# Sliding-window attention before a gated feed-forward: key blocks from token 0, and probabilities added in pairs before they are summed

## The chip, the cores and the metric

The kernel runs on one NeuronCore of a Trainium2 chip: TensorE (matrix products into PSUM), ScalarE (activations), VectorE (element by element), GpSimd (which here issues loads), SyncE (which here issues stores and DMA transposes), SBUF, and PSUM of 8 banks of 128 x 512 float32. The metric is the device time of one execution in microseconds; the median of the runs counts.

## What is computed

Eight batches of eight heads, 576 tokens, 64 values per head. A token sees itself and the 127 tokens before it, with a bias that falls with the distance. The attention output of all batches, 4608 rows of 512, goes through a feed-forward of width 1536 with a GELU gate.

```python
scores = scale * np.matmul(q, k.transpose(0, 1, 3, 2))
rel = pos[:, None] - pos[None, :]
mask = (rel >= 0) & (rel < 128)
scores = np.where(mask, scores + bias, -1e9)
attn = np.exp(scores - max) / sum
x = (attn @ v) -> rows of 512
g = x @ w_gate
out = (gelu(g) * (x @ w_val)) @ w_out
```

## The kernel before

The work order of every engine is written out by hand; a tile's buffer is handed on in the order in which buffers were released.

**Attention, per batch.** q and k stand transposed (qT, kT: values on partitions, two heads of a pair c in the two halves i of 64 rows). Key block j covers tokens 128j - 64 to 128j + 63, so block 0 is half empty, and there are five. `score` (L191) makes keys-by-queries products; two heads of a pair run side by side in TensorE. A batch is split into two parts of its queries, s = 0 (320 tokens) and s = 1 (256). `scores2` (L204) does the 128 queries of block 2 that belong to part 0, `scores` (L220) the rest, for given pairs c; each pair takes two banks. ScalarE takes the exponential (L199), VectorE multiplies by the stored mask and bias `emask` (L202). `sums` (L313 to 323) adds the probabilities over keys with a matrix of ones, four pairs in four column strips of TensorE, then a reciprocal (L323). `products` and `values` (L351, L367) make probabilities times v, and VectorE multiplies by the spread reciprocal into xT, which holds all 4608 tokens. The reciprocals are spread over 64 partitions by a float32 matmul with a selection matrix (`spread_pe`, L339, batches 1 and 2; `spread4`, batch 0) or through DRAM (`gather`, `spread_dma`, from batch 3).

**Feed-forward, per group g of 512 tokens.** `gate_val(g, f)` (L387 to 402) makes feature block f of 12: eight matmuls into two banks, GELU on ScalarE (L400), product on VectorE (L401). `out_half` (L411) makes half of 128 output rows. A gate phase is the 12 blocks; the output phase that follows runs through the list `todo[g]`, eight output halves with attention steps of batch g + 2 between them (g = 0 does the whole of batch 1; g = 1 the whole of batch 2 and the scores of batch 3). From g = 2 the sums and values of batch g + 1 lie in the gate phase (L613 to 629; for g = 2 the values lie in the output phase).

**The start.** Batch 0 and 1 are transposed by TensorE (`transpose_runs`, L153), 320 and 256 tokens of batch 0 in two loads (`RUNS`). While data comes, `keep_busy` puts in matmuls of zeros (24 of them, L70). Group 0's first seven blocks are done for tokens 0 to 319 and then 320 to 511. Weights come in four steps of columns (256, 384, 384, 512), L460 to 464.

**Queues.** GpSimd issues every load of q, k, v and weights (L101, L128, L138, L554), in order. SyncE issues the DMA transposes of batches 2 to 7 (`transposes_dma`, L185; batch 2 from `todo[0]`, the others at the head of a gate phase, L601) and the stores of the output (L424). A one-element copy, `mark`, lets GpSimd wait for something before it goes on with loads: at g = 1 (L604) for batch 3's qT, ahead of the loads of batch 4. Batch 3's q and k and batch 2's v are loaded after gate phase 0, ahead of `todo[0]` (L633), with no mark.

Of the kernel before, what the change touches and what calls it, by code (L numbers as in the profile page):

```python
# [13 lines left out]

PART = ((0, 320), (320, 576))

PIECES = (((0, 0, 192), (1, 64, 320), (2, 192, 320)),
          ((2, 0, 128), (3, 0, 256), (4, 128, 256)))  # L20


PCOL = ({0: 64, 1: 256}, {4: 0, 2: 128, 3: 256})
# [3 lines left out]
def kernel(  # L27
# [12 lines left out]
    W = 128  # L40
# [10 lines left out]
    p_pool = (ctx.enter_context(tc.tile_pool(name="pa", bufs=8)),  # L51
              ctx.enter_context(tc.tile_pool(name="pb", bufs=4)))
    p2_pool = ctx.enter_context(tc.tile_pool(name="p2", bufs=2))
# [8 lines left out]

# [19 lines left out]
    xT = consts.tile([128, 4, NTOK], BF16, name="xT")  # L82
    ident = consts.tile([128, 128], BF16, name="ident")
    ones = consts.tile([128, 2, 2, 32], BF16, name="ones")
    ones4 = consts.tile([128, 2, 8 * 36], BF16, name="ones4")
    ones8 = consts.tile([128, 4 * 36], BF16, name="ones8")
    emask = consts.tile([128, H, 256], BF16, name="emask")
# [6 lines left out]
    qT, kT = ([consts.tile([128, 5, 4, 128], BF16, name=f"{nm}T{i}") for i in range(2)]  # L94
              for nm in "qk")
    vb = [consts.tile([128, 5, DM], BF16, name=f"vb{i}") for i in range(2)]

    def load(t, src, b, js=range(5)):
        for j in js:
            lo = 64 if j == 0 else 0  # L100
            nc.gpsimd.dma_start(  # L101
                out=t[lo:128, j, :].rearrange("p (h d) -> p h d", h=H),
                in_=src[b][:, 128 * j - 64 + lo:128 * j + 64, :].rearrange("h p d -> p h d"))
# [4 lines left out]

    RUNS = (((0, 64, 5), (320, 128, 2)), ((0, 128, 3), (384, 96, 2)))

    def runs(what, b, n):
        first, parts, r = RUNS[b][n]
        t, lo, p = (qs, ks)[what][b], 1536 * n, 0
        if (b, n) == (0, 1):

            t, lo = vb[1], 512 + 1024 * what
        elif b == 0:  # L120
            p = 64 * what
        return t.rearrange("p j x -> p (j x)")[p:p + parts, lo:lo + 512 * r].rearrange(
            "p (h x) -> p h x", h=H)
# [9 lines left out]
    def load_v(b, js=range(5)):  # L133
        load(vb[b % 2], v, b, js)

# [6 lines left out]

    def by_pair(t):
        return t.rearrange("p j c t -> p (j c t)").rearrange("p (c x) -> p c x", c=4)

    def transpose_runs(b, n, what, c, ps):

        first, parts, r = RUNS[b][n]
        src = runs(what, b, n)
        p = 64 * what if (b, n) == (0, 0) else 0  # L150
        for x in range(r):
            for i in (0, 1):
                nc.tensor.transpose(  # L153
                    out=ps[64 * i:64 * i + 64, parts * x:parts * x + parts],
                    in_=src[:, 2 * c + i, 64 * x:64 * x + 64],
                    identity=ident[p:p + parts, p:p + parts])

    def untangle(copy, b, n, what, c, ps):

        first, parts, r = RUNS[b][n]  # L160
        dst = by_pair((qT, kT)[what][b])[:, c, 64 + first:64 + first + parts * r]
        if isinstance(c, int):
            copy(out=dst.rearrange("p (x r) -> p x r", r=r),  # L163
                 in_=ps[:, 0:parts * r].rearrange("p (r x) -> p x r", r=r))
        else:
            n = c.stop - c.start
            copy(out=dst.rearrange("p c (x r) -> p c x r", r=r),
                 in_=ps[:, 0:n * parts * r].rearrange("p (c r x) -> p c x r", c=n, r=r))

    def transpose(b, what, c, copy):  # L170
# [3 lines left out]
        for n, lo in ((0, 0), (1, 384)):  # L174
            untangle(copy, b, n, what, c, ps[:, lo:576])

    def blocks(t, b, i, c, j, n):
        if b < 2:
            return by_pair(t[b])[64 * i:64 * i + 64, c, 128 * j:128 * (j + n)].rearrange(
                "p (n t) -> p n t", n=n)  # L180
        return t[b % 2][64 * i:64 * i + 64, j:j + n, c, :]

    def transposes_dma(b):
        for src, dst in ((ks, kT), (qs, qT)):
            nc.sync.dma_start_transpose(  # L185
                out=dst[b % 2].rearrange("p j c t -> p (j c) t"),
                in_=src[b % 2].rearrange("p j x -> p (j x)"))

    probs, probs2 = {}, {}

    def score(b, c, i, j, qj, n, ps, col):  # L191
        nc.tensor.matmul(  # L192
            out=ps[:, col:col + 128 * n].rearrange("p (n t) -> p n t", n=n),
            lhsT=blocks(kT, b, i, c, j, 1).rearrange("p n t -> p (n t)"),
            rhs=blocks(qT, b, i, c, qj, n),
            start=True, stop=True)
# [7 lines left out]
    def scores2(b, later=None):  # L204

        P = p2_pool.tile([128, 4, 2, 128], BF16, name="P2")
        probs2[b] = P
        ps = [bank(), bank()]
        for c in range(4):
            for i in (0, 1):  # L210
                score(b, c, i, 2, 2, 1, ps[i], 128 * c)
        for i in (0, 1):
            exp(P[:, :, i, :], ps[i].rearrange("p (c n) -> p c n", c=4))
        if later is None:
            for i in (0, 1):
                mask(P[:, :, i, :], emask[:, i:8:2, 0:128])
        else:
            later.append((P.rearrange("p c i n -> p (c i) n"), emask[:, :, 0:128]))

    def scores(b, s, cs, then=None, later=None):  # L220


        pss = []
        for c in cs:
            ps = [bank(), bank()]
            pss.append(ps)
            for j, qj, n, col in (((0, 0, 2, 0), (1, 1, 2, 256)),
                                  ((4, 4, 1, 0), (2, 3, 1, 128), (3, 3, 2, 256)))[s]:
                for i in (0, 1):
                    score(b, c, i, j, qj, n, ps[i], col)  # L230
        if then:
            then()
        for c, ps in zip(cs, pss):
            P = p_pool[s].tile([128, 2, 512], BF16, name="P")
            probs[b, s, c] = P
            for i in (0, 1):
                exp(P[:, i, :], ps[i])
            args = (P.rearrange("p i (n x) -> p i n x", n=2),
                    emask[:, 2 * c:2 * c + 2, :].unsqueeze(2).to_broadcast((128, 2, 2, 256)))
# [5 lines left out]
    def prob(b, s, c, i, j, n):  # L245
        if (s, j) == (0, 2):
            return probs2[b][:, c, i, 0:n]
        return probs[b, s, c][:, i, PCOL[s][j]:PCOL[s][j] + n]

# [8 lines left out]

    WIDE = (80, 128)

    def sums0(s):
        w = WIDE[s]
        ps = bank()
        todo = []
        for c in range(4):
            for i in (0, 1):
                for j, a, e in ((0, 0, 192), (1, 64, 320)) if s == 0 else PIECES[1]:  # L270
                    todo.append((c, i, j, a, e))
        if s == 0:
            todo += [(c, i, 2, 192, 320) for i in (0, 1) for c in range(4)]
        mms = []
        for c, i, j, a, e in todo:
            for x in range(a // w, (e + w - 1) // w):
                lo, hi = max(a, w * x), min(e, w * x + w)
                g = x if s == 0 else 2 * x + c // 2
                h = 2 * c + i
                mms.append((g, ones4[:, min(j, 1), 32 * h:32 * h + 32] if s == 0 else  # L280
                            ones8[:, 32 * (h % 4):32 * (h % 4) + 32],
                            prob(0, s, c, i, j, e - a)[:, lo - a:hi - a], lo - w * x, hi - w * x))
        for n, (g, lhsT, rhs, lo, hi) in enumerate(mms):
            nc.tensor.matmul(
                out=ps[32 * g:32 * g + 32, lo:hi], lhsT=lhsT, rhs=rhs,
                start=all(m[0] != g for m in mms[:n]), stop=all(m[0] != g for m in mms[n + 1:]),
                skip_group_check=True)
        nc.vector.reciprocal(row(0)[:, PART[s][0]:PART[s][0] + w], ps[:, 0:w])

    def spread4_banks(b, s):  # L290
        lo, w = PART[s][0], WIDE[s]

        pss = [bank() for _ in range(4)]
        n = (4, 2)[s]
        for k in range(n):
            for g, ps in enumerate(pss):
                nc.tensor.matmul(
                    out=ps[:, w * k:w * k + w],
                    lhsT=sel[32 * g:32 * g + 32, 2 * k:2 * k + 2, :].rearrange("p i m -> p (i m)"),
# [4 lines left out]
    def spread4(b, s, copies):  # L304
        lo, w, n = PART[s][0], WIDE[s], (4, 2)[s]
        for g, ps in enumerate(spread4_banks(b, s)):
            c, x = ((0, g), (2 * (g % 2), g // 2))[s]
            copies[g](out=recip[b][:, c:c + n, lo + w * x:lo + w * x + w],
                      in_=ps[:, 0:n * w].rearrange("p (c x) -> p c x", c=n))

    def sums(b, s):

        ps = bank()  # L313
        for j, a, e in PIECES[s]:
            for i in (0, 1):
                for c in range(4):
                    nc.tensor.matmul(  # L317
                        out=ps[32 * c:32 * c + 32, a:e],
                        lhsT=ones[:, min(j, 1), i, :], rhs=prob(b, s, c, i, j, e - a),
                        start=(i == 0 and j == 2 * s), stop=(i == 1 and j == 2 * s + 2),  # L320
                        skip_group_check=True)
        lo, hi = PART[s]
        nc.vector.reciprocal(row(b)[:, lo:hi], ps[:, 0:hi - lo])  # L323

# [14 lines left out]
    def spread_pe(b, s, copies=(nc.scalar.copy, nc.vector.tensor_copy)):  # L339
        lo, hi = PART[s]  # L340
        pss = [bank() for _ in range(4)]
        for c, ps in enumerate(pss):
            nc.tensor.matmul(  # L343
                out=ps[:, 0:hi - lo],
# [325 lines left out]
```

The softmax here doesn't subtract the row's maximum and nothing guards it: scores larger than these inputs give would overflow.

## Time and profile before

| | |
|---|---|
| median of 6 runs | 357.83 us (357.43 to 358.87) |
| the profiled execution | 358.87 us, span 357.1 |
| TensorE, ScalarE, VectorE, GpSimd busy | 347.2, 186.0, 188.2, 103.3 us |
| TensorE's clock granted | 1.00 in nearly all of the span |
| first gate matmul, end of gate phase 0, of output phase 0 | 19.55, 46.21, 65.31 us |
| end of gate phase 1, of output phase 1 | 86.13, 107.67 us |
| a steady group (182.03 to 219.21) | 37.18 us |

The span is from the first to the last instruction on the core. A line of instructions gives start, duration and what the engine was idle for before it, with what ended the wait in brackets; "x8" merges eight instructions. A matmul's duration is longer than its distance to the next, since matmuls are pipelined.

### The profile page before, as it was taken

What the parts mean: (1) busy time and instruction counts of PE and PEld (TensorE: products, weight loads), DVE (VectorE), ACT (ScalarE), POOL (GpSimd) and SP (SyncE); (2) the same over time, 40 slices, a digit from 0 to 9 for tenths busy, and PEclk for the clock granted to TensorE, in tenths of its full rate; (3) what the DMA queues carried; (4) which work ended last, traced back from release to release, by engine and by line L of the source; (5) the groups of instructions that cost most, each with busy time, mean ns of one, the idle gap of its engine ahead of it and who ended that gap; (6) DMA issues with size and microseconds to landing.
All of it is one profiled execution on the core that took longest, in us unless ns stands there. A gap on an engine that the chain in (4) does not pass through costs nothing.

```text
span 357.1 us, 7058 instructions
## 1 busy us (share of the span) xinstructions
PE 347.2 (97%) x2827; PEld 174.7 (49%) x2868; DVE 188.2 (53%) x327; ACT 186.0 (52%) x342; POOL 103.3 (29%) x137
## 2 busy tenths in 40 slices
PE   8899999999999999999999999999999999999995
PEld 3558555444454445445454545445444444444443
DVE  4777469434888646655556554746474403403320
ACT  5784496536878366633873287337832133313322
POOL 8843569600940175002910192004000000000000
PEclk9999999999999999999999999999999999999999
DMA  7999999999999099973997499859205020011002
GB/s 91 179 196 197 201 145 194 158 153 170 140 150 180 2 184 181 160 153 63 142 204 166 85 137 194 138 132 94 87 9 132 28 92 1 2 60 57 2 29 88
DMA packets 145632, 42.62 MB, mean 119 GB/s; under 512 B 131608, under 2 KB 138520, under 8 KB 145600
## 3 DMA queue, kind: packets, MB, share of 16 engines
q0 software_dynamic: 106368, 18.88, 68.8%
q1 hardware_dynamic: 36432, 17.31, 21.6%
q10 hardware_dynamic: 2800, 5.99, 7.7%
q8 instruction: 22, 0.36, 0.4%
q14 instruction: 10, 0.08, 0.1%
HBM read 43.65 MB, written 9.53 MB: 149 GB/s over the span
## 4 chain that ended last, share of the span: by engine, by line
PE 88%; DVE 3%; DMA 3%; POOL 3%; issue 1%; ACT 0%; POOLq 0%; ACTq 0%; DVEq 0%
PE ps L394 52%; PE ps L417 24%; PE ps L360 5%; PE ps L192 4%; DMA wv<-in_moe_w_val_dram 3%; PE ps L317 2%; DVE P L202 1%; DVE r L323 1%; PE ps L431 1%; POOL vb L101 1%; POOL vb L128 0%; POOL wg L138 0%; PE ps L343 0%; POOL ks L128 0%; DVE kT L163 0%
## 5 line engine op out<-in xcount | busy, mean ns | idle before, releaser
L401 DVE TENSOR_TENSOR hT<-ps,gelu 128x512 bf16<-128x512 f32 (+2 forms) x115 | 73.8, 653 | 105.5 <-PE ps L394 90.4
L400 ACT ACTIVATE gelu<-ps 128x512 bf16<-128x512 f32 (+2 forms) x115 | 65.1, 571 | 115.9 <-PE ps L394 113.2
L394 PE MATMUL ps<-xT,wv 128*128 128x512 bf16 (+2 forms) x454 | 111.4, 366 | 1.0 <-DMA wv<-in_moe_w_val_dram 0.4
L394 PE MATMUL ps<-xT,wg 128*128 128x512 bf16 (+2 forms) x444 | 110.4, 366 | 0.9
L417 PE MATMUL ps<-wo,hT 128*128 128x512 bf16 x401 | 94.3, 380 | 1.1 <-issue 0.2
L199 ACT ACTIVATE P<-ps 128x512 bf16<-128x512 f32 x144 | 73.1, 631 | 6.9 <-PE ps L192 6.9
L394 PEld LDWEIGHTS <-wv 128*128 128x128 bf16 x460 | 44.6, 98 | 49.4 <-DMA wv<-in_moe_w_val_dram 0.8
L394 PEld LDWEIGHTS <-wg 128*128 128x128 bf16 x460 | 43.3, 98 | 47.4 <-issue 0.5
L202 DVE TENSOR_TENSOR P<-P,emask 128x1024 bf16<-128x1024 bf16 (+1 forms) x79 | 49.0, 641 | 30.2 <-ACT P L199 29.7
L417 PEld LDWEIGHTS <-hT 128*128 128x128 bf16 x420 | 38.9, 98 | 47.8 <-issue 3.7
L101 POOL DMA_DIRECT2D vb<-in_v_dram x40 | 33.9, 887 | 12.7 <-DMA ks<-in_k_dram 4.8
L422 ACT COPY osb<-ps 128x512 f32<-128x512 f32 x31 | 18.6, 601 | 32.8 <-PE ps L417 32.2
L623 POOL COPY mark<-hT 1x2 bf16<-1x2 bf16 x4 | 0.7, 175 | 96.5 <-DVE hT L401 96.5
L370 DVE TENSOR_TENSOR xT<-ps,rb 128x256 bf16<-128x256 f32 (+1 forms) x60 | 22.9, 445 | 9.4 <-DMA rb<-rd 7.0
L323 DVE RECIPROCAL r<-ps 128x320 f32<-128x320 f32 (+1 forms) x14 | 26.6, 1932 | 1.3 <-PE ps L317 1.3
L101 POOL DMA_DIRECT2D qs<-in_q_dram x30 | 25.2, 861 | 7.2 <-DMA wo<-in_moe_w_out_dram 5.1
L101 POOL DMA_DIRECT2D ks<-in_k_dram x30 | 25.4, 898 | 2.4 <-DMA qs<-in_q_dram 2.1
L192 PE MATMUL ps<-qT,kT 64*128 64x256 bf16 (+1 forms) x384 | 22.3, 244 | 1.5 <-DVE kT L163 0.6
L192 PEld LDWEIGHTS <-kT 64*128 64x128 bf16 x384 | 13.4, 94 | 13.5 <-issue 9.4
L360 PE MATMUL ps<-P,vb 128*64 128x128 bf16 (+2 forms) x384 | 18.3, 244 | 0.0
L360 PEld LDWEIGHTS <-vb 128*64 128x64 bf16 x384 | 14.6, 110 | 5.4 <-issue 4.8
L70 PE MATMUL ps<-zeros 128*128 128x512 bf16 x24 | 8.3, 476 | 1.0 <-DVE zeros L441 1.0
(73 smaller groups left out, 117.5 us busy)
## 6 DMA issues: line engine op xcount, KB each, us to landing
out_dram<-osb SPq DMA_DIRECT2D x35, 256.0 KB, 3.9
rb<-rd ACTq DMA_DIRECT2D x10, 576.0 KB, 7.4
vb<-in_v_dram POOLq DMA_DIRECT2D x32, 128.0 KB, 7.3
qs<-in_q_dram POOLq DMA_DIRECT2D x24, 128.0 KB, 5.5
ks<-in_k_dram POOLq DMA_DIRECT2D x24, 128.0 KB, 7.1
wo<-in_moe_w_out_dram POOLq DMA_DIRECT2D x2, 768.0 KB, 17.5
wg<-in_moe_w_gate_dram POOLq DMA_DIRECT2D x2, 384.0 KB, 10.8
wv<-in_moe_w_val_dram POOLq DMA_DIRECT2D x2, 384.0 KB, 11.9
```

Of the source, the lines that this page charges most:

```text
L101: nc.gpsimd.dma_start(out=t[lo:128, j, :].rearrange("p (h d) -> p h d", h=H), in_=src[b][:, 128 * j - 64 + lo:128 * j + 64, :].rearrange(" ...
L192: nc.tensor.matmul(out=ps[:, col:col + 128 * n].rearrange("p (n t) -> p n t", n=n), lhsT=blocks(kT, b, i, c, j, 1).rearrange("p n t -> p ( ...
L199: nc.scalar.activation(out=dst, in_=src, func=AF.Exp, scale=0.125)
L202: nc.vector.tensor_tensor(out=dst, in0=dst, in1=m, op=ALU.mult)
L323: nc.vector.reciprocal(row(b)[:, lo:hi], ps[:, 0:hi - lo])
L360: nc.tensor.matmul(out=ps[64 * i:64 * i + 64, a:e], lhsT=vb[b % 2][:, j, 64 * h:64 * h + 64], rhs=prob(b, s, c, i, j, e - a), start=(j == ...
L370: nc.vector.tensor_tensor(out=xT[:, c, b * S + lo:b * S + hi], in0=ps[:, 0:hi - lo], in1=recip[b][:, c, lo:hi], op=ALU.mult)
L394: nc.tensor.matmul(out=ps[:, 0:hi - lo], lhsT=w[:, c, 128 * f:128 * (f + 1)], rhs=xT[:, c, t0 + lo:t0 + hi], start=(c == 0), stop=(c == 3))
L400: nc.scalar.activation(out=gl[:, 0:hi - lo], in_=pg[:, 0:hi - lo], func=AF.Gelu)
L401: nc.vector.tensor_tensor(out=hid[g][:, f, lo:hi], in0=pv[:, 0:hi - lo], in1=gl[:, 0:hi - lo], op=ALU.mult)
L417: nc.tensor.matmul(out=po, lhsT=hid[g][:, f, 128 * t:128 * (t + 1)], rhs=wo[:, f, :], start=(f == 0), stop=(f == NF - 1))
L422: (nc.vector.tensor_copy if g < 2 and t < 2 else nc.scalar.copy)(out=osb, in_=po)
```

## The change

- Key blocks start at token 0; the last has 64 tokens. Part 0 is tokens 0 to 255, part 1 the other 320. No `scores2`; a score step covers one part of one pair in two banks, always 512 columns. For batches from 2 on (transposed by DMA in blocks) some pieces are 64 wide.
- Probabilities of a batch lie in one tile. Every query from token 128 on has keys in two blocks; `add` adds the two on VectorE, and `sums` (batches 3 to 7) or `sums4` (0 to 2; four groups of tokens in the four strips, all eight heads) sums the result. Batch 0's are summed unadded.
- Batches 1 and 2 spread with `spread4`. The scores of part 0 of batch 1 (2) and their exponentials lie beside blocks 6 to 8 of gate phase 0 (4 to 6 of gate phase 1); the GELUs of two blocks there are held until the exponentials are issued.
- `out_part` makes a quarter of 128 output rows, sixteen per group. All output copies are on ScalarE, and group 0's stores are issued from it.
- xT is a ring of 3072 tokens. Blocks of 256 columns keep gate and value in one bank.
- The start: 256 and 320 tokens, 14 matmuls of zeros, mask and identity made from one ramp by VectorE, weights in six steps of 256 columns with batch 1's rows ahead of the last two, and batch 1's transposes and first scores before block 7.
- Batch 3's q and k and batch 2's v are loaded after output phase 0, behind a mark on batch 2's qT.

```diff
-PART = ((0, 320), (320, 576))
+PART = ((0, 256), (256, 576))
+SCORES = (((0, 0, 256, 0), (1, 128, 256, 256)),
+          ((2, 256, 256, 512), (3, 384, 192, 768), (4, 512, 64, 960)),
+          ((2, 256, 256, 512), (3, 384, 128, 768), (3, 512, 64, 896), (4, 512, 64, 960)))
+PIECES = (((0, 0, 256, 0), (1, 128, 256, 256)),
+          ((2, 256, 512, 512), (1, 256, 384, 384), (3, 384, 576, 768), (4, 512, 576, 960)))
...
+    def add(b, s, cs=range(4)):
+        lo, hi = 2 * cs[0], 2 * cs[-1] + 2
+        P = prob(b).rearrange("p c i n -> p (c i) n")[:, lo:hi, :]
+        T = both[b][:, lo:hi, :]
+        def plus(out, in0, in1):
+            nc.vector.tensor_tensor(out=out, in0=in0, in1=in1, op=ALU.add)
+        if s == 0:
+            plus(T[:, :, 0:128], P[:, :, 128:256], P[:, :, 256:384])
+        else:
+            by2 = P[:, :, 384:896].rearrange("p h (n y x) -> p h n y x", n=2, y=2)
+            plus(T[:, :, 128:384].rearrange("p h (n x) -> p h n x", n=2),
+                 by2[:, :, :, 0, :], by2[:, :, :, 1, :])
+            plus(T[:, :, 384:448], P[:, :, 896:960], P[:, :, 960:1024])
...
+    WIDE = (64, 80)
+    def sums4(b, s, added=True):
+        w, first = WIDE[s], PART[s][0]
...
+        for h in range(H):
+            for g in range(4):
+                t = first + w * g
+                if added and t >= 128:
+                    mms.append((g, h, T[:, h, t - 128:t - 128 + w], 0, w))
+                else:
+                    for _, a, e, col in PIECES[s]:
+                        lo, hi = max(a, t), min(e, t + w)
+                        if lo < hi:
+                            mms.append((g, h, P[:, h, col + lo - a:col + hi - a], lo - t, hi - t))
...
+    def sums(b):
+        P, T = prob(b), both[b].rearrange("p (c i) n -> p c i n", i=2)
+        for s in (0, 1):
+            pieces = ((P, 0, 0, 128), (T, 0, 128, 256)) if s == 0 else ((T, 128, 0, 320),)
...
     load_runs(0, 0, 4, 8)
+    load_v(0, (0, 1))
     load_runs(0, 1, 0, 8)
-    load_v(0, (0, 1, 2))
     load_w(0, 256)
-    load_w(256, 640)
-    load_v(0, (3, 4))
-    load_w(640, 1024)
-    load_w(1024, DFF)
+    load_w(256, 512)
+    load_v(0, (2, 3, 4))
+    load_w(512, 768)
+    load_w(768, 1024)
     for n in (0, 1):
         load_runs(1, n, 0, 8)
+    load_w(1024, 1280)
+    load_w(1280, DFF)
...
+    scores(0, 1, (1,))
+    gate_val(0, 0, 0, 256, tails)
+    scores(0, 1, (2,))
+    gate_val(0, 1, 0, 256, tails)
+    scores(0, 1, (3,))
+    gate_val(0, 2, 0, 256, tails)
+    gate_val(0, 3, 0, 256, tails)
+    sums4(0, 1, False)
...
+    spread4(0, 1, (act, dve, act, dve))
...
+    values(0, 1)
...
     todo = {
+        0: [("s", 1, 1, (0, 1), None, masks), ("spread4", 1, 0, both_), 1, ("pv", 1, 0),
+            ("masks",), 1, ("s", 1, 1, (2,), None, masks), 1, ("s", 1, 1, (3,), None, masks),
+            ("add", 1, 1, (0, 1)), ("masks",), ("add", 1, 1, (2, 3)),
+            ("transposes", 2), 6, ("sum4", 1, 1), 2, ("spread4", 1, 1, both_), 1, ("pv", 1, 1), 4],
+        1: [("s", 2, 1, (0, 1), None, masks), ("spread4", 2, 0, both_), 1, ("pv", 2, 0),
...
+            ("s", 3, 0, (0,), None, masks), 1, ("s", 3, 0, (1,), None, masks), ("sum4", 2, 1), 1,
...
+    held = {(0, 7), (0, 8), (1, 5), (1, 6), (0, 10), (1, 8)}
+    beside = {
+        (0, 7): [("s", 1, 0, (2,))], (0, 8): [("s", 1, 0, (3,)), ("add", 1, 0), ("tails",)],
+        (0, 10): [("sum4", 1, 0), ("tails",)],
+        (1, 4): [("s", 2, 0, (0, 1))], (1, 5): [("s", 2, 0, (2,))],
+        (1, 6): [("s", 2, 0, (3,)), ("add", 2, 0), ("tails",)],
+        (1, 8): [("sum4", 2, 0), ("tails",)],
+        (2, 0): [("add", 3, 0)], (2, 1): [("add", 3, 1)],
+    }
+    scores(1, 0, (0, 1))
...
+        return [("s", b, 0, (0, 1, 2)), 6, ("s", b, 0, (3,)), ("add", b, 0),
+                ("s", b, 1, (0, 1)), ("add", b, 1, (0, 1)), 6, ("s", b, 1, (2, 3)),
+                ("add", b, 1, (2, 3)), 4]
...
-                if f == (2 if g == 2 else 0):
+                if f == (3 if g == 2 else 1):
...
         if g == 0:
             for t in (qs[1], ks[1]):
-                nc.gpsimd.memset(t[0:64, 0, :], 0.0)
+                nc.gpsimd.memset(t[64:128, 4, :], 0.0)
...
+        if g == 0:
+            nc.gpsimd.tensor_copy(out=mark, in_=qT[0][0:1, 0, 0:2])
             load_qk(3)
             load_v(2)
```

## The prediction

> **What bounds the kernel now.** I read the page's busy table first, then busy time by stage, then TensorE's timeline and the chain of waits, and last the DMA issues around the transposes.
>
> ```profile
> PE 347.2 (97%) x2827; PEld 174.7 (49%) x2868; DVE 188.2 (53%) x327; ACT 186.0 (52%) x342; POOL 103.3 (29%) x137
> ...
> PEclk9999999999999999999999999999999999999999
> ```
>
> TensorE is busy 97% of the span at full granted clock, the others about half. Busy is flattered by overlapping matmuls, so starts count, not durations:
>
> ```profile
> 111.98 1.03 PE L394 MATMUL ps<-xT,wv 128*128 128x512 bf16 x4
> 112.94 1.12 PE L317 MATMUL ps<-P,ones 128*32 128x192 bf16 x48
> 114.00 1.04 PE L394 MATMUL ps<-xT,wg 128*128 128x512 bf16 x3
> ```
>
> Four 512-column matmuls start 0.864 us apart from the next four (117.46 to 118.32 in the same timeline), so one costs 216 ns: 2.4 columns per ns plus about 3 ns. The 48 matmuls of the denominators (L317) hold TensorE from 112.94 to 114.00. They work in four column strips at once: 2432 columns in time, 1.01 us at that rate, plus some 0.05 us for the change of shape. So columns in time are the price of attention work.
>
> ```profile
> 19.55:35.09 15.54, 15.11 (x185) 11.98 (x185) 11.37 (x36) 9.32 (x23) 6.55 (x8) 1.00 1.49 195
> 46.21:65.31 19.10, 18.43 (x209) 9.64 (x209) 15.05 (x26) 14.06 (x31) 17.13 (x22) 1.00 2.04 166
> 65.31:86.13 20.82, 20.71 (x96) 9.31 (x97) 7.61 (x11) 9.07 (x15) 3.17 (x4) 1.00 1.72 170
> 86.13:107.67 21.54, 20.74 (x253) 11.02 (x257) 17.45 (x30) 18.21 (x37) 12.84 (x16) 1.00 1.48 137
> 182.03:219.21 37.18, 36.92 (x285) 18.03 (x289) 21.03 (x33) 20.87 (x37) 12.73 (x16) 1.00 1.25 149
> ```
>
> These are five stages (stretch, length, busy time of TensorE, its weight load, VectorE, ScalarE, GpSimd, then clock and DMA): seven feature blocks of group 0; output phase 0; gate phase 1; output phase 1; one steady group. The steady group holds 144 x 0.216 = 31.1 us of feed-forward and 6.1 us of attention, of which 11904 columns in time are 4.96. Nothing but columns is left to save there. Output phase 0 holds 10.4 of feed-forward and 6.0 of attention in columns (4.96 and about 1.0 for the spreads), so 2.7 of its 19.1 us is waiting; output phase 1, with 1.9 of batch 3's scores on top, waits 3.2. ScalarE shows why:
>
> ```profile
> 48.17 8.93 ACT L199 ACTIVATE P<-ps 128x512 bf16<-128x512 f32 x18
> ...
> 59.24 0.60 PE L317 MATMUL ps<-P,ones 128*32 128x128 bf16 x21 [0.39 <-DVE P L202]
> ```
>
> 18 exponentials run back to back for 8.93 us, and TensorE waits for the masks behind them. At the start the chain runs through a weight load, and later stages hang on transposes:
>
> ```profile
> 11.53 11.28 DMA wv<-in_moe_w_val_dram
> ...
> 60.45 5.60 SPq L185 DMA_TRANSPOSE kT<-ks  x1
> 66.17 8.21 SPq L185 DMA_TRANSPOSE qT<-qs  x1
> ...
> 107.71 3.43 SPq L185 DMA_TRANSPOSE kT<-ks  x1
> 111.31 3.12 SPq L185 DMA_TRANSPOSE qT<-qs  x1
> ```
>
> The q transpose of batch 2, beside running loads, landed 13.9 us after issue, at 80.1; the one at 111.31, with the queue to itself, after 6.6.
>
> **The change: columns, batches 3 to 7.** Per batch, columns in time: scores 4608 to 4096 (the separate 128-wide block falls away), sums 2432 to 1152 (pairs are added on VectorE), values 4864 to 4096 (first part 256+128 instead of 192+256+128). At 2.4 per ns: -0.21, -0.53, -0.32. From gate phase 2 on there are five sums, five value steps and four score steps left: -2.65 -1.60 -0.84 = -5.1. Against it, from batch 2 on one value piece and two score pieces per head are 64 wide; a pair streams in 27 ns and loads two weights of 36 ns pitch (0.86 us for 24 at 27.28). 128-wide pairs lost nothing: 24 value matmuls with 2560 columns took 1.01 us (27.28 to 28.29). So 0 to 45 ns on each of 12 pairs, 0 to 0.5 us per batch; I take 0.15, nearer the pairs that lost nothing: +0.6 over four batches. A gain from narrower pieces is excluded, the columns being the same. Sum **-4.5** (-5.1 to -3.1).
>
> The additions cost VectorE per batch one 1024-wide, two 512-wide and two 256-wide operations: by the mask rows 0.69 and 0.42, and some 0.29 for 256, together 2.1 us; a 1024-wide mask (0.69) goes. They stand in output phases between masks that wait for exponentials, with VectorE at 21 of 37 us; two exponentials of 0.51 us per batch leave ScalarE. I cost them at nothing; the cover is the 2.3 us at the head of a gate phase before its first GELU is done (table load 1.28 and GELU), and beyond it a delay of the reciprocals, worth at most 1 us a batch. The sums start one block (1.7 us) later, so their two reciprocals (3.76) end about 0.6 us later; the gather behind GELU 3 is issued no later than now. Nothing.
>
> **Group 1, both phases (42.4 us now).** Work after: gate phase 20.76 + batch 2's first scores 0.87 + narrow sums 0.35 + switches 0.3 = 22.3. Held GELUs: exponentials begin after block 4's GELU and a table load of 1.28, so c0 and c1 end 3.1 us after block 4, c2 4.1, c3 5.4; freed banks are reused in order of release, so block 7 (ready at 4.45) takes the banks of c2. No stall; if it took the held banks, it would wait for a GELU at 7.3, 2.9 us. Output phase: 10.4 + scores 0.85 + batch 3's 1.7 + two narrow spreads 2.0 + sums 0.4 + values 1.7 + switches 1.0 = 18.1. Waits by the same counting: VectorE's product of block 11 before the first spread 0.2, recip copies before the values 0.3, the last scores' banks 0.5, smaller ones 0.2: 19.3. The added wait: `mark` now holds batch 3's loads and batch 2's values behind batch 2's q transpose. Loads of batch 2 land by about 60 as now; transposes without other loads take 8 to 10 us instead of 20, so qT lands at 69, three us before it is needed at 72. Behind it on GpSimd's queue stand ten loads and five of values at 0.85 us: last k issue 77, landed 82; transposes of batch 3 wait for that on SyncE's queue and land at 90 to 94, beside the value loads, which land at 87 to 90. TensorE wants those values at 88 and batch 3's scores at 93.7. Wait 0 to 5 us; I take 1.0. Sum 42.6: **+0.2** (-1.0 to +4.5).
>
> **Rest of group 0 (8.8 us of blocks 7 to 11, 19.1 of output phase).** Batch 1's first scores come before block 7: table 1.28, eight exponentials of 0.51, table again, then the held GELUs at 7.7 us. Block 9 waits about 0.35 for c2's banks: 8.65 + 0.9 (scores) + 0.35 + 0.35 (sums) = 10.3. The output phase keeps 10.4 + 0.43 + 0.43 (scores) + 2.0 + 0.4 + 1.7, 0.4 of switches, and waits 0.55 for block 11's product and 0.3 for copies: 16.6. ScalarE takes two more output copies (0.6 each) and issues four DMAs; issues of 0.61 stand beside GELUs in the steady trace, so nothing, 2.4 if not. 26.9 against 27.9: **-1.0** (-2.5 to +1.5).
>
> **The start (to 35.09, and 2.3 us of batch 1's transposes).** GpSimd drops three selects (0.86 us) and VectorE makes mask and identity; narrower blocks reach the first gate matmul at 16.5 to 17 instead of 19.55. What follows is longer: 14 half blocks of 0.86, scores 0.44, sums 0.9, a reciprocal no longer covered by a block 0.7, spread 1.06, values 1.1. But DMA moves some 190 KB/us here, and weights for block 2 are the 2432nd KB instead of the 2752nd: near 20.5 instead of 22.86. TensorE would stand two us for them. From there 0.86 x 2, 0.9, 0.7, 1.1, 1.1, nine blocks and the transposes end at 36.95, against 37.4: **-0.5** (-2 if weights come early, +1.5 if batch 1's rows, 5.5 MB deep, come after 33.8).
>
> **Sum:** -4.5 +0.2 -1.0 -0.5 = -5.8 on a span of 357.1. The profiled execution took 358.87, 1.8 above its span; the median of the six is 357.83, so I say 352.0.
>
> One rule speaks against this. The Trainium skill ("TensorE: Matmul & The Clock Gate", section "Wait — 56ns, not 53.3ns?") says that matmuls never start closer than about 25 ns, however narrow. The row: 63 narrow sums (L284) fit between 13.63 and 14.41, 12 ns each. The change has 256 of them in batches 0 to 2 (48+80, and 32 in each of four parts). My stage sums hold 3.05 us for these, as the row gives; by the rule they would be 6.4, an estimate, and the total -2.4.
>
> **The rivals.**
> 1. *Batch 2's transposes land too late, slower.* If q's transpose still lands at 80.1, as now, TensorE stands in gate phase 1 from 72.0, 8.1 us, less 0 to 1 us that the later wait then saves: 359.6. It decides against the change from a landing at 77.8 on. For it: DMA is nearly full to 116 us. Against: what slowed it, the next batch's loads, is now held back. 0.15.
> 2. *Batch 3's loads are late instead.* 4 us more wait in output phase 1: 356.0. For it: 13 us of load and 8 to 12 of transposing against 25 available. 0.14.
> 3. *Weights or rows late at the start.* +2.5 us: 354.5. For it: the chain row above. Against: weights in four smaller steps come sooner. 0.08.
> 4. *The columns saved do not show,* because bank waits in every output phase give them back (4.5 us and the 1.0): 357.5. Against: the steady output phase keeps six score banks between output parts as now. 0.05.
>
> **How the numbers follow.** Forecast 0.58, its own range 349 to 354 (terms' near ends). The range 348.4 to 357.2 takes in rivals 2 and 3. Under 0.2% (0.7 us) nothing can be told from no change. Faster: 0.58+0.14+0.08; same: rival 4 less 0.01; slower: rival 1 and that 0.01.
>
> **What would show it.** Steady group 36.2 to 36.4 instead of 37.18, sums of 24 matmuls in 0.55 us; scores per steady batch 0.2 us less; gate phase 1 near 22.3 without a gap before batch 2's scores; output phase 0 near 16.6. A wait of TensorE for qT after block 4, or for vb or qT in output phase 1, tells rivals 1 and 2; a first gate matmul after 19 or a gap of over 2 us before block 2 tells rival 3. If VectorE rather than ScalarE ended the waits of TensorE in output phases, costing the additions at nothing was wrong, and with it the prediction.

## The result and the profile after

The changed kernel takes 359.62 us (median of 22 runs, 357.75 to 361.22), the kernel before 357.84 (47 runs, 357.28 to 359.23): 1.0043 times, 95% interval 1.0032 to 1.0054. It is slower by 0.4%, where 1.6% faster was forecast. The profiled execution took 358.28 us with a span of 356.5.

The page of the changed kernel: TensorE's busy time, the granted clock, the queue that brings instructions (packets, MB, share), the chain.

```profile
PE 344.8 (97%) x2890; PEld 174.1 (49%) x2930; DVE 193.6 (54%) x346; ACT 185.1 (52%) x333; POOL 105.2 (30%) x139
...
PEclk9899999999999999999999999999999999999999
...
q8 instruction: 23, 0.38, 0.4%
...
PE 95%; issue 2%; ACT 1%; DVE 1%; ACTq 0%
```

TensorE is still the bound. New is the 8 in the second slice of the clock, and "issue" is 2% of the chain, where it was 1%: time in which TensorE waits for nothing that the profile names. The slow clock lies in the start, and so do the two longest of these stops. By stage (stretch, length, busy time of TensorE, its weight load, VectorE, ScalarE, GpSimd, then clock and DMA):

```profile
18.67:40.24 21.57, 19.20 (x353) 16.11 (x350) 15.02 (x41) 13.40 (x33) 14.31 (x19) 1.00 1.57 192
50.84:67.94 17.10, 16.84 (x214) 9.42 (x217) 10.47 (x23) 8.31 (x16) 4.88 (x7) 1.00 1.42 152
67.94:90.72 22.78, 22.52 (x142) 9.80 (x144) 11.03 (x17) 15.44 (x25) 12.74 (x16) 1.00 1.60 161
90.72:111.11 20.39, 19.96 (x270) 10.85 (x274) 14.59 (x29) 16.29 (x32) 12.74 (x16) 1.00 1.53 137
184.17:220.60 36.43, 36.17 (x261) 17.44 (x264) 22.77 (x40) 19.92 (x34) 12.74 (x16) 1.00 1.15 144
```

These are the first feature blocks with batch 1's transposes, output phase 0, gate phase 1, output phase 1 and a steady group. All stages, in us of the two profiled spans:

| stage | before | forecast | after | after less forecast |
|---|---|---|---|---|
| start, to the end of batch 1's transposes | 37.4 | 36.95 | 40.24 | +3.3 |
| rest of group 0 (to 67.94) | 27.9 | 26.9 | 27.70 | +0.8 |
| group 1 (to 111.11) | 42.4 | 42.6 | 43.17 | +0.6 |
| from gate phase 2 to the end | 249.4 | 244.9 | 245.4 | +0.5 |
| span | 357.1 | 351.3 | 356.5 | +5.2 |

The medians add 2.4 us to that: the profiled run of before lay 1.0 us above its median, the one of after 1.3 below. The gain in the later groups came; the start gave most of it back. TensorE's timeline there (start, duration, what ended the idle time):

```profile
10.21 0.83 PE L198 MATMUL ps<-qT,kT 64*128 64x256 bf16 x8 [1.25 <-DVE kT L158]
...
16.46 0.45 PE L319 MATMUL ps<-r,sel 32*128 32x64 f32 x7 [0.49 <-issue]
...
18.67 0.61 PE L415 MATMUL ps<-xT,wg 128*128 128x256 bf16 x4
...
23.14 1.04 PE L308 MATMUL ps<-P,ones 128*32 128x80 bf16 x80
24.93 1.13 PE L319 MATMUL ps<-r,sel 32*128 32x80 f32 x32 [0.76 <-DVE r L312]
26.00 1.30 PE L372 MATMUL ps<-P,vb 128*64 128x256 bf16 x32
27.23 0.28 PE L415 MATMUL ps<-xT,wg 128*128 128x256 bf16 x1
29.13 0.49 PE L415 MATMUL ps<-xT,wg 128*128 128x256 bf16 x3 [1.61 <-issue]
```

Three things are to be seen: a wait of 1.25 us for VectorE ahead of the scores of pairs 2 and 3; a stop of 0.49 us inside the spread; and a stop of 1.61 us inside block 4, whose first matmul had run, so its input and first weights were there. The clock around the first of them (same columns as the stages):

```profile
7.00:10.00 3.00, 1.59 (x47) 0.81 (x41) 2.97 (x8) 1.64 (x4) 3.00 (x5) 1.00 1.61 129
10.40:13.70 3.30, 3.30 (x60) 1.65 (x58) 2.34 (x6) 2.52 (x7) 2.44 (x3) 0.50 1.28 174
```

From 10.29 to 13.70, 3.41 us long, TensorE ran at half clock; from 7.00 to 10.00 it had been busy for 1.59 of 3 us. Behind that the clock is full again. Run to run this differs: of the changed kernel's runs that list a clock, six with a mean of 0.995 have spans of 356.0 to 356.8, seven at 0.986 have 357.6 to 358.4, six at 0.980 have 358.1 to 359.4 (the other four lie between, at 0.981 to 0.990). 3.41 us at half clock is 0.0048 of the span, so these are one, three and four such windows. In the 60 runs of before that list a clock its mean was 0.998 or more.

### The profile page after: what moved, and what is told of

It reads as the page before. It is cut to its first block, busy times and chain, and to the rows that moved or that the text cites. A ratio compares the mean times of both kernels' runs of the same rounds, so it can differ in the third digit from the quotient of the medians.

```text
span 356.5 us, 7121 instructions
## 1 busy us (share of the span) xinstructions
PE 344.8 (97%) x2890; PEld 174.1 (49%) x2930; DVE 193.6 (54%) x346; ACT 185.1 (52%) x333; POOL 105.2 (30%) x139
## 4 chain that ended last, share of the span: by engine, by line
PE 95%; issue 2%; ACT 1%; DVE 1%; ACTq 0%
PE ps L415 52%; PE ps L441 26%; PE ps L198 5%; PE ps L372 5%; PE ps L319 2%; PE ps L71 2%; PE ps L150 1%; PE ps L308 1%; PE ps L342 1%; PE ps L455 1%; ACT L202 0%; DVE kT L158 0%; ACT P L202 0%; DVE sel L499 0%; ACT kT L158 0%
## 5 line engine op out<-in xcount | busy, mean ns | idle before, releaser
L422 DVE TENSOR_TENSOR hT<-ps,gelu 128x512 bf16<-128x512 f32 (+1 forms) x115 | 73.9, 653 | 98.2 <-PE ps L415 87.2
L421 ACT ACTIVATE gelu<-ps 128x512 bf16<-128x512 f32 (+1 forms) x115 | 64.6, 572 | 108.1 <-PE ps L415 102.1
L415 PE MATMUL ps<-xT,wg 128*128 128x512 bf16 (+1 forms) x449 | 111.4, 366 | 2.2 <-issue 1.6
L415 PE MATMUL ps<-xT,wv 128*128 128x512 bf16 (+1 forms) x447 | 110.4, 366 | 0.5
L202 ACT ACTIVATE P<-ps 128x512 bf16<-128x512 f32 (+1 forms) x130 | 66.4, 606 | 11.8 <-PE ps L198 11.7
L446 ACT COPY osb<-ps 128x512 f32<-128x512 f32 x35 | 20.9, 598 | 37.4 <-PE ps L441 33.1
L386 DVE TENSOR_TENSOR xT<-ps,rb 128x320 bf16<-128x320 f32 (+2 forms) x64 | 23.6, 433 | 8.4 <-DMA rb<-rd 4.7
L198 PE MATMUL ps<-qT,kT 64*128 64x256 bf16 (+3 forms) x376 | 21.6, 240 | 1.9 <-DVE kT L158 1.6
L347 DVE RECIPROCAL r<-ps 128x256 f32<-128x256 f32 (+1 forms) x10 | 18.8, 1921 | 0.0
L372 PE MATMUL ps<-P,vb 128*64 128x128 bf16 (+3 forms) x384 | 17.8, 242 | 0.1
L271 DVE TENSOR_TENSOR S<-P 128x1024 bf16<-128x1024 bf16 (+3 forms) x33 | 17.1, 551 | 0.6
```

What stands on the lines that cost most here:

```text
L198: nc.tensor.matmul(out=out, lhsT=columns(kT, b, i, c, 128 * j, 128), rhs=rhs, start=True, stop=True)
L202: nc.scalar.activation(out=dst, in_=src, func=AF.Exp, scale=0.125)
L372: nc.tensor.matmul(out=ps[64 * i:64 * i + 64, a - lo:e - lo], lhsT=vb[b % 2][:, j, 64 * h:64 * h + 64], rhs=P[:, c, i, col:col + e - a], s ...
L386: nc.vector.tensor_tensor(out=xT[:, c, at:at + e - a], in0=ps[:, a - lo:e - lo], in1=recip[b][:, c, a:e], op=ALU.mult)
L415: nc.tensor.matmul(out=ps, lhsT=w[:, c, 128 * f:128 * (f + 1)], rhs=xT[:, c, t0 + lo:t0 + hi], start=(c == 0), stop=(c == 3))
L421: nc.scalar.activation(out=gl[:, 0:n], in_=pg, func=AF.Gelu)
```

## What was tried

Theories after the result: **C**, the start has gaps in which the clock falls to half, in more windows in the median run than in the profiled one; **V**, VectorE's order (mask copy and selection matrix ahead of what TensorE needs) makes the first gap; **F**, the 1.61 us is TensorE waiting for its own instructions; **S**, that stop is the wait for the sums or something else tied to its place.

**Zeros in the gaps (e1_warm).**

```diff
+    keep_busy(2)
     scores_first((0, 1), second)
+    keep_busy(5)
     scores_first((2, 3))
-    keep_busy(2)
+    keep_busy(3)
     products_first((0, 1), act)
...
     for tail in tails[:3]:
         tail()
+    keep_busy(3)
     spread4(0, 1, (act, dve, act, dve))
```

> The changed kernel with 11 more matmuls of zeros (25 instead of 14) in TensorE's waits of the start: 2 before the first scores, 5 before the scores of pairs 2 and 3, one more before the first values, 3 before the second spread. Clock theory: its runs differ because the granted clock falls to half for one or more windows of 3.4 us after the 1.25 us idle at 9 to 10.2 us; with the wait filled the mean clock is 0.998 or more in every run, the spread of the runs falls from 3.5 us to about 1.5, and the median is 2 us lower, near 357.5. Rival, that the runs differ for another reason (transfers): clock and median stay, about 359.6 plus what the zeros cost. On the 1.8 us pause before block 4: if it is the fetch of TensorE's instructions, it comes again after 479 matmuls, so earlier in the program, among the values of part 1, and still ends near 29 us; if it belongs to block 4 (its weights), it stays ahead of block 4.

357.97 us (12 runs, 356.49 to 359.25), 0.9995 of before (0.9979 to 1.0011): 1.65 us under the changed kernel. Five of 12 runs were granted 0.999 or more, with a mean span of 355.4. The profiled one was not. Its timeline, and the clock behind that first wait:

```profile
12.14 0.50 PE L150 MATMUL ps<-ident,ks 64*64 64x64 bf16 x20 [1.22 <-DMA ks<-in_q_dram]
...
28.72 0.50 PE L372 MATMUL ps<-P,vb 128*64 128x64 bf16 x10 [0.65 <-issue]
```

```profile
14.30:20.90 6.60, 6.60 (x102) 5.25 (x100) 3.99 (x9) 3.99 (x8) 3.54 (x5) 0.50 1.76 183
```

The gap for VectorE is filled, and one for k's rows takes its place; two half-clock windows follow. The issue stop came 10 value matmuls before their end, where it had been behind them: 22 instructions earlier, as many as the 11 zeros add. That speaks for a count of instructions and against block 4.

**VectorE's order (e2_dve_order).**

```diff
-    nc.vector.tensor_copy(out=emask[:, 0:4, 256:384], in_=emask[:, 0:4, 0:128])
-    made_later()
...
     def second():
...
+        nc.vector.tensor_copy(out=emask[:, 0:4, 256:384], in_=emask[:, 0:4, 0:128])
         nc.vector.tensor_copy(out=emask[:, 4:8, 256:384], in_=emask[:, 4:8, 0:128])
...
     scores_first((2, 3))
+    made_later()
```

> The changed kernel with three VectorE operations moved behind the transposed copies of pairs 2 and 3: the copy of the mask for heads 0 to 3 (0.65 us) and the two that make the selection matrix (0.19 and 0.74). VectorE theory: the scores of pairs 2 and 3 start at about 8.9 instead of 10.2 us, the idle 1.25 us goes, and with it the fall of the clock; first block of the feed-forward 1.5 to 2.5 us earlier, median 2 to 4 us lower. Fetch theory as a rival for most of it: the later pause ends at a time that the fetch sets (near 29 us in the profile), so what is gained before it is waited for there, and only the clock's part shows: block 4 no more than 1 us earlier.

359.64 us (6 runs), 1.0057 of before (1.0036 to 1.0078), no better than the changed kernel. One run, the profiled one, had the full clock and a span of 355.5; the other five were granted 0.980 to 0.986 with 357.6 to 359.1. In it TensorE still waits for the transposed copies, the first gate matmul starts 1.03 us sooner, and the stop is the same:

```profile
9.29 0.67 PE L198 MATMUL ps<-qT,kT 64*128 64x256 bf16 x8 [0.90 <-DVE kT L158]
...
17.64 0.61 PE L415 MATMUL ps<-xT,wg 128*128 128x256 bf16 x4
...
28.09 0.49 PE L415 MATMUL ps<-xT,wg 128*128 128x256 bf16 x3 [1.61 <-issue]
```

V is right that the order makes part of the wait (0.90 us instead of 1.25), but no gain in the total is shown for it. The microsecond of the profiled run may be the half-clock window, which after has and this run has not. At equal clock the runs do not differ: three at 0.986 have spans of 357.6 to 357.9, within those of after, and at full clock e1_warm without this order (355.4) equals e6_dve_warm with it (355.45).

**Fewer matmuls in the sums (e3_add_first).** Batch 0's later sums from added probabilities: 96 fewer weight loads and matmuls in the trace.

```diff
+    add(0, 1, (0, 1))
     scores(0, 1, (3,))
+    add(0, 1, (2, 3))
...
-    sums4(0, 1, False)
+    sums4(0, 1)
```

> The changed kernel with batch 0's part 1 also added in pairs on VectorE before it is summed: 32 narrow matmuls instead of 80, so 96 fewer TensorE instructions (with their weight loads) ahead of the pause before block 4. Fetch theory: the 479th matmul then falls some three to six half blocks later, its instructions are there in time, and the pause of 1.8 us goes or shrinks below 0.5; the additions delay the denominators by 0.5, net 1.0 to 1.5 us less. Rival, the pause belongs to block 4's weights or tokens: it stays at 1.5 us or more after the values, and the kernel gains nothing.

360.89 us (6 runs), 1.0082 of before (1.0064 to 1.01), with 0.981 granted in all six.

```profile
26.04 0.51 PE L308 MATMUL ps<-S,ones 128*32 128x80 bf16 x16 [0.91 <-DVE S L271]
...
29.11 2.25 PE L372 MATMUL ps<-P,vb 128*64 128x256 bf16 x32
31.28 0.61 PE L415 MATMUL ps<-xT,wg 128*128 128x256 bf16 x4
```

The stop is gone, block 4 follows the values. But the additions on VectorE are now waited for, and four half-clock windows (three from 10.64 to 20.88, one from 27.71) cost more than it saved.

**The kernel before with 14 zeros instead of 24 (e4_before_cold).**

```diff
-    keep_busy(4)
-    scores(0, 0, (0, 1), lambda: (keep_busy(2), first((2,)), first((3,))))
-    keep_busy(2)
+    scores(0, 0, (0, 1), lambda: (first((2,)), first((3,))))
...
-    keep_busy(4)
+    keep_busy(2)
```

> The kernel before with 14 matmuls of zeros instead of 24: those before the scores of pairs 0 and 1, inside them and before pairs 2 and 3 are left out, two fewer before the remaining transposes. Clock theory: TensorE then idles 1 us or more between 7 and 12 us, the clock falls for one or more windows in some or most runs (mean clock 0.98 to 0.995 instead of 0.999), the median rises by 1 to 3 us and the runs spread over 3 us. Rival, zeros only fill time: median unchanged within 0.3 us or a little lower.

357.79 us (12 runs), 1.0002 of before (0.9988 to 1.0016). Half of the runs lost clock (0.990 to 0.995), and their spans (355.8 to 357.9) are on the mean 0.6 us longer than the others' (355.6 to 356.0). The median stays. Fewer zeros alone do not explain the result: a window of half clock costs the kernel before little there.

**Batch 2's exponentials back in the output phase (e5_late_exp).**

```diff
-        1: [("s", 2, 1, (0, 1), None, masks), ("spread4", 2, 0, both_), 1, ("pv", 2, 0),
-            ("masks",), 1, ("s", 2, 1, (2,), None, masks), 1, ("s", 2, 1, (3,), None, masks),
-            ("add", 2, 1, (0, 1)), ("masks",), ("add", 2, 1, (2, 3)), 4,
+        1: [("s", 2, 0, (0, 1)), 2, ("s", 2, 0, (2, 3)), ("add", 2, 0), 2,
+            ("s", 2, 1, (0, 1), None, masks), ("sum4", 2, 0), 1, ("spread4", 2, 0, both_),
+            ("pv", 2, 0), ("masks",), ("s", 2, 1, (2,), None, masks), 1,
+            ("s", 2, 1, (3,), None, masks),
+            ("add", 2, 1, (0, 1)), ("masks",), ("add", 2, 1, (2, 3)), 1,
...
-    held = {(0, 7), (0, 8), (1, 5), (1, 6), (0, 10), (1, 8)}
+    held = {(0, 7), (0, 8), (0, 10)}
```

> One part of the change undone, for batch 2 alone: its part 0 scores, exponentials and narrow sums leave gate phase 1 and lie in output phase 1 again. If exponentials beside the gate phase hide what ScalarE otherwise makes TensorE wait for (as the prediction had it), gate phase and output phase of group 1 together grow from 43.2 us to 44.2 to 45.7, and the median to 360.6 to 362. Rival, that TensorE has as much cover for them in the output phase: 43.2 within 0.4 us, median unchanged. Start and steady groups stay in both.

364.38 us (4 runs), 1.018 of before (1.016 to 1.02). Group 1 takes 48.2 us (68.78 to 116.98) instead of 43.17, more than either theory said. TensorE waits for the added probabilities, and then the clock falls (timeline, then stage columns):

```profile
96.27 0.21 PE L308 MATMUL ps<-S,ones 128*32 128x64 bf16 x2 [2.03 <-DVE S L271]
```

```profile
96.60:103.30 6.70, 6.14 (x73) 3.82 (x66) 3.70 (x9) 2.35 (x6) 5.48 (x7) 0.51 2.04 162
```

Without the exponentials beside the gate phase this group loses 5 us, of which the two half-clock windows behind one wait (6.83 us at half clock, up to 3.4 lost) are a large part. So nothing speaks for that part of the change as a cause of the loss. How much ScalarE time it hides is not shown, since the order put in its place is a poor one: the kernel before did the same work in another order, without additions ahead of the sums, in 42.4.

**VectorE's order and zeros together (e6_dve_warm).** The edit of e2_dve_order and these:

```diff
+    keep_busy(2)
     scores_first((0, 1), second)
+    keep_busy(4)
     scores_first((2, 3))
...
-    keep_busy(2)
+    keep_busy(3)
     products_first((0, 1), act)
+    keep_busy(4)
     rest(0, (0, 1), act)
```

> The changed kernel with both earlier edits together: the copy of the masks and the selection matrix later on VectorE, and eleven more matmuls of zeros in the waits of the first 13 us. If the rest of the changed kernel's median lies in the clock (windows of half clock that come or not from run to run) and in VectorE's order, every run is granted 0.995 or more, and the median is 355.5 to 357, two to three us under the changed kernel. The stop behind 961 weight loads and matmuls stays, 0.6 to 1.6 us, since their number does not fall. If the clock is not what separates the runs, the median stays at 358 or above while the granted clock rises.

357.44 us (12 runs), 0.9989 of before (0.9972 to 1.0007). Ten of 12 runs were granted 0.999 or more, mean span 355.45: that is e2_dve_order's one full-clock span (355.5), in nearly every run (the other two were granted 0.994, where 0.995 was expected of all). 2.2 us of median between the two, from matmuls of zeros alone, is C shown. The expected 355.5 to 357 was missed by 0.4. The same stretch as in e1_warm, and the stop:

```profile
14.30:20.90 6.60, 6.46 (x149) 5.02 (x144) 4.71 (x11) 5.51 (x12) 3.68 (x6) 1.00 1.76 183
```

```profile
28.11 0.50 PE L372 MATMUL ps<-P,vb 128*64 128x64 bf16 x10 [1.81 <-issue]
```

149 matmuls in the 6.6 us that held 102 at half clock. The stop stays.

**Fewer instructions, and block 4 ahead of the spread (e7_fewer_reordered).** On top of e6_dve_warm; the 4 in `sums4` means that heads 0 to 3 are summed from the added probabilities, the others from the unadded:

```diff
+    add(0, 1, (0, 1))
     scores(0, 1, (3,))
...
-    sums4(0, 1, False)
+    sums4(0, 1, 4)
     for tail in tails[:3]:
         tail()
+    gate_val(0, 4, 0, 256, tails)
     spread4(0, 1, (act, dve, act, dve))
...
     values(0, 1)
-    gate_val(0, 4, 0, 256)
```

> As the run before, and half of batch 0's later sums made from added probabilities (48 instructions of TensorE fewer), and feature block 4 between those sums and the spread. If TensorE stops where 256 of its instructions have gone in less than about 6 us, the stop behind the values falls under 0.4 us, and block 4 covers the wait for the reciprocal (0.76 us): block 7 near 38.0 instead of 40.78, median 353.5 to 355.5. Rival, that what comes late at this place is a weight or a bank: block 4 waits for it in its new place, and the median is within 0.5 us of the run before.

356.15 us (6 runs), 0.995 of before (0.9932 to 0.9969): faster than both kernels.

```profile
24.30 0.61 PE L415 MATMUL ps<-xT,wg 128*128 128x256 bf16 x4 [0.84 <-DMA wg<-in_moe_w_gate_dram]
25.59 0.61 PE L415 MATMUL ps<-xT,wv 128*128 128x256 bf16 x4 [0.69 <-DMA wv<-in_moe_w_val_dram]
```

The stop and the wait for the reciprocal are gone: the spread (26.14), the values and block 5 (28.44) follow without one. Block 4's weights are now late: the rival was right about what comes next, and the median missed the expected band by 0.65. Batch 1's transposes end at 39.03 (39.77 in e6_dve_warm). That the stop is gone shows less than it seems here: with the waits for weights the 256 instructions took 6.4 us (22.56 to 29.00).

**The stop's place alone (e8_shift).**

```diff
+    ps = bank()
+    for n in range(66):
+        nc.tensor.matmul(out=ps[:, 0:8], lhsT=zeros, rhs=zeros[:, 0:8], start=True, stop=True)
     keep_busy(9)
```

> The changed kernel with 66 matmuls of 8 zero columns ahead of the first zeros, where TensorE has nothing to do: 132 instructions more, no work moved. If the stops come at counts of instructions (449 and 961), the 1.6 us behind batch 0's values are gone, and TensorE stops, for 0.5 us or more, about 130 instructions earlier: among the transposes and scores ahead of the first feature block, and about at the wait for the reciprocal. The stage ends within 1 us of before. Rival, that the stop belongs to its place (weights, a bank, the loads): 1.6 us behind the values as before.

359.55 us (7 runs), 1.0049 of before (1.003 to 1.0069): the changed kernel's median.

```profile
19.84 0.58 PE L198 MATMUL ps<-qT,kT 64*128 64x256 bf16 x5 [0.53 <-issue]
...
29.98 1.30 PE L372 MATMUL ps<-P,vb 128*64 128x256 bf16 x32
31.22 0.61 PE L415 MATMUL ps<-xT,wg 128*128 128x256 bf16 x4
```

Nothing behind the values any more; TensorE stops among scores ahead of the first block instead. The expected stop at the reciprocal did not come, and three half-clock windows (15.53 to 25.77) put this profiled start 2.2 us behind, where at most 1 was expected. F is shown: no work was moved, and the stop went with the count. Moving it alone gains nothing.

**Weights first (e9_weights_first), and block 5 too (e10_block5_too).** On top of e7_fewer_reordered; the second has both edits.

```diff
-    load_v(0, (2, 3, 4))
     load_w(512, 768)
+    load_v(0, (2, 3, 4))
```

```diff
+    gate_val(0, 5, 0, 256)
     values(0, 1)
-    gate_val(0, 5, 0, 256)
```

> As the run with fewer instructions and block 4 ahead of the spread, and the weights of blocks 4 and 5 loaded ahead of the last three blocks of v. There TensorE waited 1.53 us for those weights in block 4. If 256 instructions of TensorE take at least about 5.9 us while loads fill the DMA engines, the weights come in time but a stop of 0.8 to 1.4 us comes back at 961 weight loads and matmuls, among or behind the values, and the median falls by 0.2 to 0.8 us, to 355.4 to 356.0. Rival, that only the weights were late: no stop, and 1.5 us less, 354.6.

> As the run before, and feature block 5 ahead of the values too: 16 instructions that take 0.87 us in place of as many that take 0.4. By the pace of instructions the stop at 961 gets 0.4 to 0.6 us shorter and the median lies another 0.3 to 0.6 us lower, near 355.2; if nothing stops there, both runs are equal.

355.63 us (12 runs), 0.9945 of before (0.9926 to 0.9963), and 355.81 (6 runs), 0.9938 (0.9925 to 0.995): not to be told apart, and both 1.1% under the changed kernel. Mean spans at full clock are 353.6 and 354.1 (354.4 in e7_fewer_reordered). In the first, with batch 1's transposes ending at 37.52:

```profile
25.50 1.31 PE L372 MATMUL ps<-P,vb 128*64 128x256 bf16 x32
26.75 0.61 PE L415 MATMUL ps<-xT,wg 128*128 128x256 bf16 x4
```

The time is as expected, the stop of 0.8 to 1.4 us is not there. My figure of 5.9 us for 256 instructions was no constant. In the second the stop comes at the count before:

```profile
16.32 0.77 PE L319 MATMUL ps<-r,sel 32*128 32x64 f32 x18 [1.54 <-issue]
```

All issue stops of the start, counted in the traces (weight loads and matmuls together, and two synchronizing instructions ahead of the first):

| kernel | stopped behind | from, to (us) | 256 earlier passed at | packet on q8 began |
|---|---|---|---|---|
| before | 449 | 14.22, 14.94 | 8.72 | 12.55 |
| after | 449 | 15.75, 16.46 | 11.94 | 14.18 |
| after | 961 | 27.24, 29.13 | 23.27 | 26.76 |
| e1_warm | 961 | 27.83, 28.72 | 24.40 | 26.26 |
| e2_dve_order | 449 | 14.38, 15.43 | 10.49 | 13.01 |
| e2_dve_order | 961 | 26.21, 28.09 | 22.24 | 25.72 |
| e5_late_exp | 961 | 28.72, 29.97 | 24.86 | 27.51 |
| e6_dve_warm | 961 | 26.05, 28.10 | 22.48 | 25.62 |
| e8_shift | 705 | 18.91, 19.84 | 14.04 | 17.38 |
| e9_weights_first | 449 | 14.52, 14.96 | 9.44 | 12.53 |
| e10_block5_too | 449 | 14.51, 16.32 | 9.44 | 13.98 |

Every stop is behind 449, 705 or 961, 256 apart, and ends 2.3 to 2.5 us after a packet of the instruction queue began. Whoever uses 256 instructions in less than the time it takes to get the next, stops: 4.3 to 6.9 us here; without a stop they went in 4.86 us in e9_weights_first and in 4.75 in e10_block5_too, where the packet began in time. In between, the packet takes 1.9 to 4.5 us to begin. That it waits behind loads, which fill the DMA engines in this stretch, fits but was not tested by itself.

## Why the prediction was wrong

- *Columns, batches 3 to 7*: right. -4.5 forecast, -4.0 measured from gate phase 2 on; the steady group 36.43 against 36.2 to 36.4; the 24 sums 0.61 us (187.72 to 188.33) against 0.55.
- *The start* failed: -0.5 forecast, +2.85 measured. Block 2 started at 21.29, without a wait for its weights, which were forecast for 20.5 (320 KB less at the text's own 190 KB/us make 21.2; in e2_dve_order they were there at 20.70, in e7_fewer_reordered at 21.11). What the timeline shows ahead of it are the wait for VectorE, the stop of 0.49 and the half-clock window. From there "0.86 x 2, 0.9, 0.7, 1.1, 1.1", the blocks and the transposes came out as worked out to within some 0.7 us, but for 1.8 us of the second stop. (The text says nine blocks; its 36.95 holds the ten that there are.) No term stood for TensorE's own instructions, though before has the same kind of stop in its list of waits, shorter and once:

```profile
PE ps L284 <- issue: 0.5, 1, 0.5
```

  The change brings more: narrow sums, half blocks and 32 more transposes put some 960 weight loads and matmuls ahead of 29.13, where before had about 860.
- *The clock* had no term. Ten matmuls of zeros fewer were costed at nothing without naming their cover, and so were the gaps that they left. In the profiled run this is one window inside the start; the median run has three, and is 1.3 us longer than the profiled one.
- *Rest of group 0* and *group 1*: -1.0 and +0.2 forecast, -0.2 and +0.8 measured. The term that was mis-sized is "two narrow spreads 2.0". Those of batch 1 after, and the wide ones of before:

```profile
51.38 1.49 PE L319 MATMUL ps<-r,sel 32*128 32x64 f32 x32
...
62.29 1.13 PE L319 MATMUL ps<-r,sel 32*128 32x80 f32 x32
63.58 0.59 PE L441 MATMUL ps<-wo,hT 128*128 128x512 bf16 x2 [0.16 <-issue]
```

```profile
57.81 0.82 PE L343 MATMUL ps<-r,sel 32*128 32x320 f32 x8
...
62.29 0.71 PE L343 MATMUL ps<-r,sel 32*128 32x256 f32 x8
```

  To the next start the narrow ones hold TensorE for 1.42 and 1.29 us (1.07 in the start, 24.93 to 26.00), the wide ones for 0.75 and 0.64. In group 1 the two narrow ones take 1.41 and 1.43 (91.27 to 92.68, 101.95 to 103.38). The 1.0 us set against loads there was not needed, and hid this error of 0.8.
- *Additions on VectorE at nothing*: right in the steady groups: from 112 us on TensorE's list of waits names no VectorE. In e3_add_first and e5_late_exp they are waited for.
- Rivals 1 and 2 fell. The q transpose of batch 2 and the k transpose of batch 3 (issues on SyncE's queue):

```profile
62.30 5.38 SPq L171 DMA_TRANSPOSE qT<-qs  x1
82.88 4.28 SPq L171 DMA_TRANSPOSE kT<-ks  x1
```

  q of batch 2 landed at 70.2 (forecast 69), needed at 76.67; the first of batch 3 was issued at 82.88 (forecast 82), its q landed at 92.36, needed at 99.08. Rival 3's late weights did not come either. Rival 1's 359.6 is the measured median to the digit, by luck: nothing of its wait of 8.1 us came. Rival 4 fell as well, since the columns do show.
- The rule that was weighed against the trace, a floor of about 25 ns for each matmul, does not hold for the packed ones here: the 32 sums at 60.49 took 0.40 us, 12.5 ns each, as the row of before had said.
- What is left: e9_weights_first, at full clock and with no idle stop above 0.2 us, is still 3.6 us above the forecast of 352.0. Its stages (ends at 37.52, 65.23, 108.39, 353.8) lie 0.6, 0.8, 0.6 and 0.5 above the forecast ones. The other 1.1 is reckoning: the stages were those of a run of before that was 1.0 above its median, and the whole gain over that run was taken off the median.

## What to carry to other kernels

Count instructions as well as columns where TensorE's work is cut into narrow pieces while loads fill the DMA: an issue stop in the trace of before, however short, says that this resource is near its bound. A gap in an otherwise busy start can cost, beyond its length, one or more windows at half clock, so zeros that fill gaps are part of the critical path, to be costed when they go. Look at the clock of every run, not at the profiled one alone: a kernel whose profile looks better than its median has a clock that comes and goes.

## What the runs showed of the hardware

- The half clock comes in stretches of 3.41, 6.83 or 10.24 us, one to three times the same length. The Trainium skill ("TensorE: Matmul & The Clock Gate", section "What's actually happening") gives a free-running window of 3413 ns, and the traces agree. The same page ("Why this matters for your kernels") warns of idle gaps from about 3 us on; here 1.25 us (after) and 2.03 us (e5_late_exp) were followed by half clock, while e2_dve_order's profiled run kept the full clock behind 0.90 and 0.83. From 7.00 to 10.00, ahead of the first, TensorE was busy for 1.59 us. In which windows the other runs of the changed kernel lost clock is not known: runs list a mean alone.
- TensorE gets its instructions in pieces of 256: all eleven stops lie 256 apart in the count, and each ended 4.3 to 6.9 us after the boundary before, while loads ran.
- A sparse stretch can be cheap: the kernel before lost clock in half of e4_before_cold's runs, and these were 0.6 us longer on the mean, with the median unchanged.
